# Attention of two of four batches by 32-query chunks instead of 64-query blocks

## The chip, the core and the metric

The kernel runs on one core of one Trainium2 chip. The metric is the time on the device in microseconds (us). An execution has five engines that run side by side: TensorE (PE, with its weight loads shown apart as PEld), VectorE (DVE), ScalarE (ACT), GpSimd (POOL) and SyncE (SP, which here only issues transfers). Each takes its instructions strictly in the order in which the program gives them; engines wait for one another by semaphores.

## The reference

Four batches, 8 heads, 768 positions, head width 64. Queries go in chunks of 32: a chunk sees 8 memory keys, the 16 positions before it, its own 32 and the 8 after it, cut off at the two ends of the sequence. After the attention comes a Fourier mixing over positions and model width, then a two-layer MLP on the normalised sum.

```
for c in range(24):                                   # chunk 32, left 16, right 8
    keys = [mem_k (8), k[max(0, 32c-16) : min(768, 32c+40)]]
    a = softmax(q[32c:32c+32] @ keys.T / 8);  x[32c:32c+32] = a @ [mem_v (8), v[same]]
u = x + real(fft(fft(x, axis=1), axis=2))
un = (u - mean) / sqrt(var + 1e-6)
out = u + relu(un @ w_ch1) @ w_ch2                    # 512 -> 2048 -> 512
```

## The kernel before

**Order of the work.** The program is a list of some hundreds of tasks, each with an engine, a cost in us, the tasks it needs (`after`), the buffers it takes and gives back, and a rank. A planner (`Plan.order`, L114) plays them through by these costs and writes one fixed order per engine; `shortest` (L1432) draws 24 slightly shuffled rankings and keeps the one whose planned end is earliest. So any change of a cost or a dependence reorders every engine. `behind=` says that a task may only be placed once another one has been placed; `lag` lets it be placed that long before its inputs are expected. MLP matmuls have the lowest rank, so they fill what the attention and Fourier tasks leave free on PE.

**Attention.** A task group `attention(n)` (L972) handles one pair of heads; n = 4b to 4b+3 are the four pairs of batch b. In batches 0 to 2, q and k are loaded by POOL's queue (`e_load_qk`, L368), turned by PE (`e_turn_q`, `e_turn_k`) and copied out of PSUM; in batch 3 (`TURNED`) they are loaded in two transfers each of 128-byte pieces and turned by transfers on SP's queue (`e_flip_q`, L408, `e_flip_k`). `e_kT` (L438) spreads k into `kTb`: 12 blocks of 64 queries, each with a column of 128 key slots: 32 unused, 8 memory keys, 88 context keys. `e_scores` (L454) does six blocks of both heads, 12 matmuls of 64 rows by 128 columns with 64 query columns moving; the two heads sit on the two row halves of the array and write to different PSUM banks. `e_exp` (L465) makes two activations of it, one for each 32-query half, with a bias that masks the keys that half may not see. `e_values` (L473) multiplies the exponentials (128 keys by 64 queries, fp32, as weights) by the value rows (65 columns: 64 and a column of ones that gives the sum), 12 matmuls for each half of the pair, two column halves of the array in turn. `e_norm` (L489) divides. Scores and exponentials run twice a pair, values once with 24 matmuls.

**Values.** `e_load_v` (L380) fills one of four buffers `va` in seven transfers on SP's queue, in rows of 256 bytes: 64 + 80 x 11 + 8 x 11 + 8 x 12 = 1,128 rows a head.

**After the attention of a batch** come `e_rows_out` on POOL's queue (L591), `e_rows_turn` on SP's (L595, the task `t_x2`) and `e_mirror` on POOL's (L600, `t_xr`), which bring half of the rows back in reverse order, and beside them the Fourier chain on DVE, ACT and PE (`fourier(b)`: zy L517, pq L524, ff L534, hi L542, lo L547, rows L557, columns L727, sums and statistics L733 to L742), the normalised rows `un` (L752) and their transposes by SP (`e_flip`, L776). Then the MLP of the batch runs in three thirds: layer 1 (`e_ch1`, L803, then relu L812) and layer 2 (L821; in batches 2 and 3 by products with sums on DVE, L858, L870, L875). The loads for batch 3 stand behind transfers of batches 1 and 2 by `behind=` in `attention`.

Of the kernel before, what the change touches and what calls it, by code (L numbers as in the profile page):

```python
# [11 lines left out]
FP32 = mybir.dt.float32  # L12
BF16 = mybir.dt.bfloat16
# [4 lines left out]
CHUNK = 32  # L18
# [4 lines left out]
MEM0 = 32  # L23
OWN = MEM0 + NMEM + LEFT


# [11 lines left out]
class Plan:  # L38
# [18 lines left out]
    def add(self, engine, cost, emit, after=(), take=(), give=(), rank=None, moved=0.0,  # L57
            loose=False, late=0.0, filler=False, behind=None, lag=0.0, pick=None, grain=0.1, head=1.0):
        t = dict(engine=engine, cost=cost, emit=emit, after=[a for a in after if a is not None],
                 take=take, give=give, rank=len(self.tasks) if rank is None else rank,  # L60
                 moved=moved, done=None, at=None, no=len(self.tasks), loose=loose,
                 late=late, filler=filler, behind=behind, lag=lag, pick=pick, grain=grain, head=head)
        self.tasks.append(t)
        return t
# [50 lines left out]
    def order(self):  # L115
# [9 lines left out]
        while any(waiting.values()):  # L125
# [5 lines left out]
            for e, ts_ in waiting.items():  # L131
# [3 lines left out]
                for t in ts_:  # L135
# [4 lines left out]
                    if any(a["done"] is None  # L140
# [3 lines left out]
                        continue  # L144
                    if t["behind"] is not None and t["behind"]["at"] is None:
                        continue
# [59 lines left out]
def kernel(  # L206
# [18 lines left out]
    NHT = DFF // P  # L225
    NT = S // 64
    RB = 8
# [42 lines left out]
    kU = [spool.tile([P, KR + S + KR], BF16, name=f"kU{i}") for i in range(NKU)]  # L270
    kTb = [spool.tile([P, NT, P], BF16, name=f"kTb{i}") for i in range(NKT)]

# [23 lines left out]
    sv = cpool.tile([P, 3], FP32)  # L296
    svS = cpool.tile([P, 3], FP32)
    svD = cpool.tile([P, 1], FP32)
    zero = cpool.tile([P, 1], FP32)
# [5 lines left out]
    mhalf = cpool.tile([P, NST], FP32)  # L305
    mbias = cpool.tile([P, 2], FP32)
    NEG = -BIGM / 8.0
# [20 lines left out]
    def e_masks():  # L328
        nc.gpsimd.memset(mbias, 0.0)
        nc.gpsimd.memset(mbias[96:128, 0:1], NEG)  # L330
        nc.gpsimd.affine_select(out=mbias[:, 1:2], in_=mbias[:, 1:2], compare_op=ALU.is_ge,
                                fill=NEG, base=-(OWN - LEFT + CHUNK), pattern=[[0, 1]],
                                channel_multiplier=1)
        nc.gpsimd.memset(mbias[0:MEM0, 1:2], 0.0)
        nc.gpsimd.memset(mbias[MEM0:MEM0 + NMEM, 1:2], 0.0)
# [11 lines left out]
    def e_edge_ones(i):  # L347
        v1 = va[i]
        lo, hi = v1[32:64, :, 0, D:D + 1], v1[96:128, :, NT - 1, D:D + 1]
        nc.gpsimd.affine_select(out=lo, in_=lo, compare_op=ALU.is_ge, fill=0.0, base=32 - OWN,  # L350
                                pattern=[[0, 2], [0, 1]], channel_multiplier=1)
        nc.gpsimd.affine_select(out=hi, in_=hi, compare_op=ALU.is_ge, fill=0.0,
                                base=OWN + 63 - 96, pattern=[[0, 2], [0, 1]],
                                channel_multiplier=-1)
        nc.gpsimd.memset(v1[MEM0:MEM0 + NMEM, :, 0, D:D + 1], 1.0)

    def e_low_rows(i):
# [22 lines left out]
    def e_load_v(n):  # L380
# [3 lines left out]
        def run(p0, count, t0, nt, key, hh):  # L384
# [3 lines left out]
                                      ap=[[D, count], [64 * D, nt], [1, D]]))  # L388

        nc.sync.dma_start(v1[OWN:OWN + 64, :, 0, 0:D],  # L390
                          v[b, 2 * pr:2 * pr + 2, 0:64].rearrange("h p d -> p h d"))
# [42 lines left out]
    def e_mkT(n):  # L434
        b, pr = seq[n]
        (nc.scalar.copy if n == HP else nc.vector.tensor_copy)(
            kTb[n % NKT][:, :, MEM0:MEM0 + NMEM],
            mkT[:, b * HP + pr, :].unsqueeze(1).to_broadcast([P, NT, NMEM]))  # L438

    def e_kT(n, eng=None):  # L440
        if n >= TURNED * HP:
            win = LEFT + 64 + RIGHT
            nc.vector.tensor_copy(
                strided(kTb[n % NKT], MEM0 + NMEM, [[P, NT], [1, win]]),
                strided(kU[n % NKU], KR - LEFT, [[64, NT], [1, win]]))
            return
        trk = tr_of.pop((n, 1))
        (eng or nc.scalar.copy)(
            strided(kTb[n % NKT], MEM0 + NMEM, [[P, NT], [RB, 11], [1, RB]]),
            strided(trk, 0, [[64 // RB, NT], [1, 11], [KP, RB]]))  # L450
        if n < HP:
            let_go(trk)

    def e_scores(n, g):  # L454
        qT, kT = qT_of[n], kTb[n % NKT]
        sc_of[n, g] = sc = aps.tile([P, 2, 8, 64], FP32, tag="sc", bufs=1, name="sc")
        for t6 in range(6):
            t = 6 * g + t6
            for hh in range(2):
                r0 = 64 * hh  # L460
                nc.tensor.matmul(sc[:, hh, t6, :], kT[r0:r0 + 64, t, :],  # L461
                                 qT[r0:r0 + 64, ts(t, 64)], start=True, stop=True,
                                 tile_position=(r0, 0))

    def e_exp(n, g):  # L465
# [41 lines left out]
    mid32 = cpool.tile([P, NST, 1], FP32)  # L507
    warm = cpool.tile([P, 1], FP32)
    xd, xt = (nc.dram_tensor(name, [2, 3, P, DM], FP32).ap() for name in ("x_rows", "x_back"))
    od = nc.dram_tensor("out_rows", [2, 3, P, DM], FP32).ap()  # L510
    gate = cpool.tile([P, 1], FP32)

# [403 lines left out]
    for i in range(NV):  # L916
# [4 lines left out]
                       rank=(0, 1, 2, 3)[i])  # L921
    t_masks = add("POOL", 0.86, e_masks, rank=16)
    dz = cpool.tile([P, P], BF16)
    fill_of = []
# [43 lines left out]

    t_used = {}

    def attention(n):
# [5 lines left out]
                      take=(("qs", "ks")[i],), moved=3.1 if b >= TURNED else 1.2, grain=0.032 if b >= TURNED else 0.1, late=LATE if b else 2.0,  # L977
                      behind=t_gate if n == HP else t_xr[b - 2] if n == TURNED * HP else t_ck.get(n - 1),
                      rank={0: -4 + i, 1: -1.2 + 0.1 * i, 2: 10 + 0.1 * i}.get(n)) for i in range(2)]
        lv = add("SP", 2.5, lambda: e_load_v(n), [t_ones[n] if n < NV else None, t_used.get(("va", n % NV))],  # L980
                 behind=t_x2.get(b - 2),
                 take=("va",), moved=2.6, grain=0.031, head=0.4, late=(0.0, 4.0, LATE, LATE)[b])
        t_lv[n] = lv
        t_ck[n] = lk
        if n == HP - 1:
# [13 lines left out]
        else:  # L999
# [6 lines left out]
                     take=(ktag,), give=("ks",))  # L1006
            ek = add(dve[0], 1.25 if dve[1] else 1.04, lambda: e_kT(n, dve[1]), [tk, mk],
                     give=(ktag,))
        t_used[0, at], t_used[1, at] = (eq, tk) if b >= TURNED else (tq, tk)
        xs_ = []  # L1010
        for g in range(2):
# [75 lines left out]
    for i in range(2, NV):  # L1087
        t_low[i]["behind"] = t_exp[i - 2, 1]
        t_low[i]["rank"] = t_exp[i - 2, 1]["rank"] + 0.1
# [85 lines left out]
    def fourier(b):  # L1175
        t_x1 = add("POOL", 1.0, lambda: e_rows_out(b), [t_norm[b * HP + i, 1] for i in range(HP)],
                   moved=2.0)
# [29 lines left out]
        return columns_of(b, t_rest)  # L1207

    t_flips = {}

# [199 lines left out]

    t_lv[14]["behind"] = t_x2[TURNED - 1]
    t_lv[15]["behind"] = t_x2[TURNED - 1]

# [33 lines left out]
```

## Time and profile before

| | us |
|---|---|
| runs | 280.25, 280.53, 280.58 (median 280.53) |
| the profiled execution | 280.87 |
| its span, first to last instruction | 279.2 |
| PE busy in the span | 264.8 (95%) |
| DVE, ACT, POOL busy | 192.6 (69%), 154.7 (55%), 63.5 (23%) |
| scores, L461: PE busy, 384 matmuls | 11.6 |
| values, L485: PE busy, xa and xo, 384 records each | 15.4 and 14.5 |
| exponentials, L469: ACT busy, 64 of 580 ns | 33.6 |
| granted TensorE clock | 1.00 |

The profile is one execution. A group's "busy" counts overlapped instructions once, its mean is the latency of one. A matmul's end is modelled and includes the way through the array, so how fast matmuls follow each other is read from starts: in the timeline a run of x records that lasts t and whose single one lasts m has its last start at t - m. One fp32 matmul leaves two records.

### The profile page before, as it was taken

To read this page: it belongs to the slowest core of one execution; us is meant where nothing else is said; L and a number is where in the kernel's file an instruction comes from. 1 tells how busy PE (TensorE), PEld (TensorE's weight loads), DVE (VectorE), ACT (ScalarE), POOL (GpSimd) and SP (SyncE) were. 2 spreads that over 40 slices of the span, in tenths; PEclk is the share of its full clock that TensorE was granted. 3 is DMA by queue.
4 is the path that set the end of the run, shared out by engine and by line. 5 is a ranking of instruction groups with operands and counts; after the bars stand their busy time and mean duration, and the time that the engine had idled before them with its cause. 6 is when DMAs were issued, how large, how long until landed. Compare 5 with 4: busy or idle time off the path is not lost.

```text
span 279.2 us, 7959 instructions
## 1 busy us (share of the span) xinstructions
PE 264.8 (95%) x3318; PEld 208.3 (75%) x3318; DVE 192.6 (69%) x424; ACT 154.7 (55%) x262; POOL 63.5 (23%) x127
## 2 busy tenths in 40 slices
PE   0599999999999999999999999999999999999995
PEld 0387797888765668758767857668889888888884
DVE  7968999941238999999937851259987975353444
ACT  6888647788777527636653556328164191605150
POOL 8852572330201096050211130001100130000000
PEclk9999999999999999999999999999999999999999
DMA  5998999999998999979992586824842057303152
GB/s 95 209 177 159 184 191 203 196 198 194 197 198 216 122 226 165 139 193 156 268 162 78 109 137 178 152 78 137 98 183 40 0 96 149 97 38 77 54 100 76
DMA packets 116116, 39.98 MB, mean 143 GB/s; under 512 B 104560, under 2 KB 111472, under 8 KB 116080
## 3 DMA queue, kind: packets, MB, share of 16 engines
q1 hardware_dynamic: 93888, 23.54, 45.6%
q0 software_dynamic: 21472, 15.21, 33.3%
q10 hardware_dynamic: 720, 0.72, 0.7%
q8 instruction: 26, 0.43, 0.7%
q14 instruction: 10, 0.08, 0.1%
HBM read 37.36 MB, written 13.37 MB: 182 GB/s over the span
## 4 chain that ended last, share of the span: by engine, by line
PE 82%; DVE 6%; POOL 5%; DMA 2%; ACT 2%; issue 2%; POOLq 0%; DVEq 0%
PE ph L803 26%; PE pc L821 15%; PE pc L870 11%; PE ps L557 6%; PE pm L727 5%; PE xa L485 4%; PE xo L485 4%; PE ps L716 3%; PE sc L461 3%; DMA qs<-in_q_dram 2%; PE trq L405 2%; PE trk L405 1%; PE idle L930 1%; ACT un L752 1%; PE pm L608 1%
## 5 line engine op out<-in xcount | busy, mean ns | idle before, releaser
L803 PE MATMUL ph<-unT,w_sb 128*128 128x256 f16 x768 | 90.0, 273 | 0.2 <-ACT hT L812 0.2
L812 ACT ACTIVATE hT<-ph 128x512 f16<-128x512 f32 x96 | 56.8, 597 | 47.3 <-PE ph L803 27.5
L803 PEld LDWEIGHTS <-w_sb 128*128 128x128 f16 x768 | 73.6, 98 | 10.8 <-issue 0.8
L821 PE MATMUL pc<-w_sb,hT 128*128 128x512 f16 x192 | 44.7, 380 | 0.0
L469 ACT ACTIVATE e<-sc,mbias 128x384 f32<-128x384 f32 x64 | 33.6, 580 | 17.7 <-PE sc L461 17.7
L821 PEld LDWEIGHTS <-hT 128*128 128x128 f16 x192 | 17.6, 98 | 19.2 <-issue 0.2
L870 PEld LDWEIGHTS <-hT 128*128 128x128 f16 x240 | 23.3, 98 | 3.9 <-issue 1.0
L875 DVE TENSOR_TENSOR xsb<-pc,xsb 128x256 f32<-128x256 f32 x43 | 17.8, 420 | 9.6 <-PE pc L870 8.4
L870 PE MATMUL pc<-w_sb,hT 128*128 128x256 f16 x192 | 24.1, 273 | 0.2 <-DVE xsb L875 0.2
L828 DVE SCALAR_TENSOR_TENSOR xsb<-pc,rstd,xsb 128x512 f32<-128x512 f32 x12 | 9.0, 749 | 18.8 <-PE pc L821 18.8
L569 ACT CAST up<-ps 128x386 f16<-128x386 f32 x16 | 9.7, 603 | 21.4 <-PE ps L557 20.4
L741 DVE BATCH_NORM_STATS2 st<-xsb 128x6 f32<-128x512 f32 x24 | 16.5, 687 | 0.5
L858 DVE TENSOR_TENSOR S<-hT 128x768 f16<-128x768 f16 (+1 forms) x12 | 5.1, 424 | 16.4 <-ACT hT L812 15.8
L485 PEld LDWEIGHTS xa<-va,e 128*64 128x64 f32 x384 | 13.1, 143 | 3.6 <-issue 2.9
L485 PE MATMUL xa<-va,e 128*64 128x65 f32 x384 | 15.4, 232 | 0.0
L752 ACT ACTIVATE un<-xsb,rs 128x512 f16<-128x512 f32 x12 | 9.5, 807 | 10.1 <-POOL rs L767 10.1
L485 PE MATMUL xo<-va,e 128*64 128x65 f32 x384 | 14.5, 227 | 0.0
L461 PEld LDWEIGHTS <-kTb 64*128 64x128 bf16 x384 | 7.7, 97 | 8.0 <-issue 5.3
L485 PEld LDWEIGHTS xo<-va,e 128*64 128x64 f32 x384 | 13.0, 142 | 0.4 <-ACT ff L651 0.3
L542 ACT CAST hi<-ff 128x768 f16<-128x768 f32 x12 | 9.9, 830 | 4.9 <-DVE ff L534 4.7
L461 PE MATMUL sc<-qT,kTb 64*128 64x64 bf16 x384 | 11.6, 196 | 0.9 <-POOL va L345 0.9
L870 PE MATMUL pc<-w_t,S 128*128 128x256 f16 x96 | 11.6, 272 | 0.4 <-DVE xsb L875 0.4
(168 smaller groups left out, 442.3 us busy)
## 6 DMA issues: line engine op xcount, KB each, us to landing
va<-in_v_dram SPq DMA_DIRECT2D x32, 220.0 KB
w_sb<-in_moe_w_ch_dram POOLq DMA_DIRECT2D x8, 512.0 KB, 14.5
out_dram<-xsb SPq DMA_DIRECT2D x12, 256.0 KB
qs<-in_q_dram POOLq DMA_DIRECT2D x12, 192.0 KB, 6.7
ks<-in_k_dram POOLq DMA_DIRECT2D x12, 192.0 KB, 6.7
x_rows<-xsb POOLq DMA_DIRECT2D x3, 768.0 KB, 4.6
xr<-x_back POOLq DMA_DIRECT2D x3, 768.0 KB, 6.0
out_rows<-xsb SPq DMA_DIRECT2D x9, 256.0 KB
```

The source lines that it names most:

```text
L461: nc.tensor.matmul(sc[:, hh, t6, :], kT[r0:r0 + 64, t, :], qT[r0:r0 + 64, ts(t, 64)], start=True, stop=True, tile_position=(r0, 0))
L469: nc.scalar.activation(e1[:, :, :, ts(half, 32)], sc[:, :, 0:6, ts(half, 32)], AFT.Exp, bias=mbias[:, half:half + 1], scale=1.0 / math.sqr ...
L485: nc.tensor.matmul(xa[64 * half:64 * half + 64, st, hh, 0:65], e1[:, hh, t6, :], v1[:, hh, 6 * g + t6, 0:65], start=True, stop=True)
L557: nc.tensor.matmul(out_[:, sp, :], part[:, ab, sp * 3 + st, c0:c1], tab[:, sp, st, :], start=(st == 0 and i == 0), stop=(st == 2 and i == 1))
L727: nc.tensor.matmul(pm[:, par, :], lhs, rhs[:, par, :], start=(im == 0), stop=(im == 3))
L741: nc.vector.bn_stats(st6, xs[b][:, kt, :])
L752: nc.scalar.activation(un, xs[b][:, kt, :], AFT.Identity, bias=rs[:, 1:2], scale=rs[:, 0:1])
L803: nc.tensor.matmul(ph[:, k, :], w1_sb[:, dt, ts(HH * k + i, P)], unT_of[b, j][:, dt, :], start=(dt == 0), stop=(dt == NDT - 1))
L812: nc.scalar.activation(hT_of[b, j][:, :, i, :], ph, AFT.Relu, bias=0.0, scale=1.0 if b in EVEN else -1.0)
L821: nc.tensor.matmul(pc_of[b, j, r], hT_of[b, j][:, k, i, ts(r, P)], w2_sb[:, HH * k + i, :], start=(i + k == 0), stop=(i + k == HH))
L870: nc.tensor.matmul(pc_of[key], a[:, i, :], w[:, i, :], start=(i == 0 and new), stop=(i == HH - 1), skip_group_check=not new)
L875: nc.vector.tensor_tensor(u, pc, u, ALU.add)
```

## The change

For the pairs n >= 8 (`FINE`: batches 2 and 3) the unit is the chunk of 32 queries with 64 keys: 56 context and 8 memory keys.

- **Scores and exponentials.** 48 matmuls of 64 by 64 with 32 columns moving, in one task; even and odd chunks go to the two partition halves. One activation over 768 columns without bias. The keys lie chunk after chunk with the memory keys between two windows, so that an odd chunk has them after its window, an even one before.
- **Values.** 48 fp32 matmuls with 64 rows by 32 columns of weights; eight in a row go to eight different places of the array. Both heads of one 128-row tile no longer share a bank: head 0 goes to xa, head 1 to xo. The norm is by head.
- **Value loads.** For each head two runs of 56-row windows and one of the memory rows (kept twice in a scratch tensor that two transfers on ACT's queue write at the start): 56 x 24 + 16 x 12 = 1,536 rows a head. At the first and last pair one window more is loaded apart. The windows of the two end chunks reach past the sequence; POOL multiplies these blocks by 0 or 1 (`e_cut`), and PE's values wait for that.
- **New small tasks.** `e_edge` on POOL once, `e_ones` on ACT once for each of the four buffers before its first use by batch 2.
- **Order of loads.** The q and k loads of n = 14 also stand behind `t_xr[2]`; the value load of 12 stands behind the last `e_flip` of batch 1, those of 13, 14 and 15 behind `t_x2[2]` (before: 12 and 13 behind `t_x2[1]`, 14 and 15 behind `t_x2[2]`).

```diff
-    kTb = [spool.tile([P, NT, P], BF16, name=f"kTb{i}") for i in range(NKT)]
+    kTf = [spool.tile([P, NCH * 64 + NMEM], BF16, name=f"kTb{i}") for i in range(NKT)]
+    kTb = [x[:, 0:NT * P].rearrange("p (t k) -> p t k", k=P) for x in kTf]
...
+    def e_cut(n):
+        ends = va[n % NV][:, :, 0:NT:NT - 1, 0:D + 1]
+        nc.gpsimd.tensor_tensor(ends, ends, edge.unsqueeze(3).to_broadcast([P, 2, 2, D + 1]), ALU.mult)
...
+        if n >= FINE:
+            for hh in range(2):
+                lo, hi = ((0, 64 + NMEM), (64 + NMEM, 0))[hh]
+                alone = hh == 0 and pr == 0
+                run(lo, WIN, alone, NT - alone, 64 * alone - LEFT, hh)
+                if alone:
+                    run(lo + LEFT, WIN - LEFT, 0, 1, 0, hh)
+                alone = hh == 1 and pr == HP - 1
+                run(hi, WIN, 0, NT - alone, CHUNK - LEFT, hh)
+                if alone:
+                    run(hi, WIN - RIGHT, NT - 1, 1, S - CHUNK - LEFT, hh)
+                two = mem2[b, 2 * pr + hh].rearrange("i m d -> (i m) d")
+                nc.sync.dma_start(v1[WIN:WIN + 2 * NMEM, hh, :, 0:D],
+                                  two.unsqueeze(1).to_broadcast([2 * NMEM, NT, D]))
+            return
...
+    def half_of(c, hh):
+        return 64 * ((c + hh) % 2)
+
+    def f_scores(n):
+        sc_of[n] = sc = aps.tile([P, 2, 16, CHUNK], FP32, tag="sc", bufs=1, name="sc")
+        for c in range(NCH):
+            for hh in range(2):
+                r0, p0 = 64 * hh, half_of(c, hh)
+                k0 = 64 * c + (0 if p0 else NMEM)
+                nc.tensor.matmul(sc[p0:p0 + 64, hh, c // 2, :], kT[r0:r0 + 64, k0:k0 + 64],
+                                 qT[r0:r0 + 64, ts(c, CHUNK)], start=True, stop=True,
+                                 tile_position=(r0, p0))
+
+    def f_exp(n):
+        nc.scalar.activation(e1, sc[:, :, 0:NT, :], AFT.Exp, scale=1.0 / math.sqrt(D))
+
+    def f_values(n):
+        for st in range(NST):
+            for c4, hh in ((0, 0), (1, 0), (2, 0), (3, 0), (1, 1), (0, 1), (3, 1), (2, 1)):
+                c = 4 * st + c4
+                p0, c0 = half_of(c, hh), CHUNK * c4
+                nc.tensor.matmul(xa[hh][c0:c0 + CHUNK, st, 0:65],
+                                 e1[p0:p0 + 64, hh, c // 2, :], v1[p0:p0 + 64, hh, c // 2, 0:65],
+                                 start=True, stop=True, tile_position=(p0, c0))
...
     def attention(n):
-                      behind=t_gate if n == HP else t_xr[b - 2] if n == TURNED * HP else t_ck.get(n - 1),
+                      behind=[t_gate if n == HP else None if n == TURNED * HP else t_ck.get(n - 1)] + [{"x": t_xr, "v": t_lv}[k].get(i) for k, i in {12:[('x',1)],14:[('x',2)]}.get(n, ())],
...
-                 behind=t_x2.get(b - 2),
-                 take=("va",), moved=2.6, grain=0.031, head=0.4, late=(0.0, 4.0, LATE, LATE)[b])
+                 behind=[{"x": t_x2, "m": t_xr, "v": t_lv, "f": {z: t_flips[z][5] for z in t_flips}}[k].get(i) for k, i in {12:[('f',1)],13:[('x',2)],14:[('x',2)],15:[('x',2)]}.get(n, ())],
+                 take=("va",), moved=3.7 if fine else 2.6, grain=0.031, head=0.4, late=(0.0, 4.0, LATE, LATE)[b])
+        if fine:
+            cut = add("POOL", 0.55, lambda: e_cut(n), [lv, t_edge], lag=CUT)
...
+        if fine:
+            s_ = add("PE", 0.45, lambda: f_scores(n), [eq, ek], take=("sc",), give=("qT", "kTb"))
+            x_ = add("ACT", 0.98, lambda: f_exp(n), [s_], take=("e1",), give=("sc",))
+            v_ = add("PE", 0.95, lambda: f_values(n), [x_, cut], take=("xa",), pick=vp, give=("e1", "va"))
...
-    t_lv[14]["behind"] = t_x2[TURNED - 1]
-    t_lv[15]["behind"] = t_x2[TURNED - 1]
```

## The prediction

> **What bounds the kernel.** I read the page first: busy shares, the 40 slices, the chain.
>
> ```profile
> PE 264.8 (95%) x3318; PEld 208.3 (75%) x3318; DVE 192.6 (69%) x424; ACT 154.7 (55%) x262; POOL 63.5 (23%) x127
> ...
> PE   0599999999999999999999999999999999999995
> ...
> PE 82%; DVE 6%; POOL 5%; DMA 2%; ACT 2%; issue 2%; POOLq 0%; DVEq 0%
> ```
>
> PE is at 9 tenths in every slice from the third to the last but one, at full clock; no other engine is. So after some 14 us every microsecond of PE work counts, as long as there is other PE work to put in its place. The same by stage (columns: window, its length, then busy us of PE, PEld, DVE, ACT, POOL, each with its instruction count, clock, DMA share, GB/s):
>
> ```profile
> 70.00:115.00 45.00, 45.00 (x752) 31.95 (x752) 32.88 (x64) 28.12 (x46) 13.40 (x18) 1.00 1.25 187
> 115.00:147.00 32.00, 31.77 (x275) 22.66 (x273) 26.45 (x48) 18.37 (x31) 6.49 (x8) 1.00 1.12 185
> 147.00:187.00 40.00, 40.00 (x471) 27.45 (x469) 18.91 (x43) 18.69 (x32) 4.73 (x12) 1.00 0.54 118
> 187.00:235.00 48.00, 47.43 (x445) 41.87 (x442) 41.94 (x89) 23.05 (x38) 5.71 (x14) 1.00 0.47 102
> 235.00:277.00 42.00, 40.95 (x371) 36.01 (x369) 18.73 (x45) 14.33 (x24) 0.00 (x0) 1.00 0.31 76
> ```
>
> Attention of batches 2 and 3 lies in the first three. The DMA engines are full until 147 (share over 1, as packets of several queues overlap), then half so. From 187 to 235 PE does the MLP of batch 2 beside the Fourier part of batch 3, in which DVE is nearly as full as PE. From 235 on only the MLP of batch 3 is left.
>
> **What PE gives for one pair now.** The last pair, in the timeline of PE (start, length, line, count):
>
> ```profile
> 180.40 0.35 PE L461 MATMUL sc<-qT,kTb 64*128 64x64 bf16 x12
> 180.68 1.90 PE L821 MATMUL pc<-w_sb,hT 128*128 128x512 f16 x8
> 182.51 0.35 PE L461 MATMUL sc<-qT,kTb 64*128 64x64 bf16 x12
> 182.79 0.61 PE L821 MATMUL pc<-w_sb,hT 128*128 128x512 f16 x2
> ...
> 185.49 0.92 PE L485 MATMUL xa<-va,e 128*64 128x65 f32 x24
> 186.24 0.87 PE L485 MATMUL xo<-va,e 128*64 128x65 f32 x24
> 187.04 0.50 PE L803 MATMUL ph<-unT,w_sb 128*128 128x256 f16 x3
> ```
>
> One score block holds PE from 180.40 to 180.68: 0.28. One of its matmuls lasts 0.19 (the tile's median), so the twelfth starts at 0.16; two run side by side on the row halves, so one place takes a matmul every 0.16/5.5 = 0.029, and 0.12 goes into leaving the block. Entering costs too: a pc matmul lasts 0.38, so the last one ahead starts at 180.68 + 1.90 - 0.38 = 182.20 and the block at 182.51, 0.31 later, against 0.61 - 0.38 = 0.23 between two pc matmuls: 0.09, rounded up. Two blocks: 2 x 0.37 = 0.74. The values hold PE from 185.49 to 187.04: 1.55. In the second half 24 records have their last start at 0.87 - 0.22 = 0.65; two column halves side by side give 12 slots, 0.65/11 = 0.058 each, and the way out costs 0.80 - 12 x 0.058 = 0.10.
>
> **What it gives after.** Scores: 48 matmuls on four places, 12 slots. A slot costs at most the 0.029 of now (the moving columns are halved) and at least half of it: 0.17 to 0.35, plus 0.12 and 0.09, in all 0.38 to 0.56. I take 0.49, nearer the known row. Saved 0.25. Values: 96 records on eight places, 12 slots. The trace has two row halves side by side (scores) and two column halves (values), not both at once nor four columns. If all eight run side by side: 0.75 as for the first half now, 0.05 until the eighth place has started, 0.10 to leave, 0.90; saved 0.65. If only two do: 48 slots, 1.55 + 24 x 0.058 = 2.94; lost 1.39. If four do: 24 slots as now; saved nothing. I take eight, since each kind of halving shows its full gain alone and the streams of one place keep their length (65 columns, 0.058). The sum is 8 pairs x (0.25 + 0.65) = 7.2 us of PE.
>
> Two rules of the Trainium skill speak against it. The first: "TensorE: Matmul & The Clock Gate" (Part 1) states that start-to-start never falls below about 25 ns, however small a matmul is. In the rows above twelve score matmuls start within 0.16 us, 14 ns apart, so here it can hold for one place only; were it one floor for all, 48 + 96 starts would by estimate take 3.6 us a pair against the 2.29 of now, and the sum would be some 10 us slower than before. The second: "TensorEngine Tiling (Array Packing)", Gotcha 1 (PSUM Pressure), states that different row tiles cannot access the same PSUM bank at the same time. No run here shows it: the scores keep each row half in its own bank, but the new values write each bank from both row halves, in different column quarters. If that serialises, four places run side by side and only the scores' 2.0 us are left.
>
> **The other engines.** ACT: four exponentials of 0.580 (128x384) become one of 768 columns; the cast L542 of 768 takes 0.83, so about 0.9: 1.4 saved a pair. ACT is not full (28, 18 and 19 us of 45, 32, 40), so this is latency: the second score block and its exponentials, 182.51 - 180.40 = 2.1 us, leave the way from k to values. `e_kT` grows from 1,056 to 1,344 columns: 0.28 more on ACT (1.04 a copy), 0.12 more on DVE (0.425), and memory-key copies double (0.22): beside that, nothing. The norm keeps its sizes (0.557 and 0.187). `e_ones` and the two scratch transfers stand early on ACT, with a buffer free at 52 us whose load is issued at 68.6: nothing; without that room 0.3 us each.
>
> `e_cut` has no equal in the trace. POOL's 128x2 power takes 0.71, its 128x800 memset 0.77, a 128x3 sum 0.35: between 0.3 and 1.5 us, 0.7 taken. It lies between landing and values; value loads of the last pairs are issued by 88 (values at 112) and by 161.5 (values at 185.5), so it has some 15 us of cover even after a landing of 7 (q and k loads take 6.7 to 7.7 from issue). Behind it on POOL wait q and k loads, x_rows and the mirror; more of that among the rivals.
>
> **Loads.** A pair's value rows rise from 2,256 to 3,072. Queue q1 takes 45.6% of 279.2 = 127 us for 93,888 packets, so 8 x 816 more cost about 8.9 us of all DMA engines, half of it before 147 where they are full. Against that two value loads (2 x 2,256 packets, 6 us) and the q, k loads of n = 14 leave that stage. One issue fewer a pair on SP (0.3 to 0.6) is nothing. Batch 3's loads now all come after 140, when x_rows of batch 2 is turned: 3 x 3,072 value rows and 4 x 1,536 rows of q and k are 15,400 packets, at 93,888/127 = 739 a microsecond 21 us, so until about 161. Before, the last k was flipped by SP at 169.1 and value load 15 issued by 161.5. So the loads come about when they came: 0, between 5 us earlier and 8 later for the attention's end.
>
> **The sum.** PE is relieved by 7.2 us before 187. From there the filler has to last: the first third of batch 3's MLP starts at 235.14, and the transposes it needs are issued at
>
> ```profile
> 228.05 2.53 SPq L776 DMA_TRANSPOSE unT<-un  x2
> ```
>
> the first of these two ends its issue near 229.3; with some 2 us to land (estimate; plain transfers take 4.6 to 7.7 from issue) it is there at about 231, 4 us before PE comes to it. With the 2.1 us by which the last attention gets shorter, 6 us of PE's lead can be used: the smaller of 7.2 and 6.1, so 6.0. 280.87 - 6.0 = 274.9 for the profiled execution; the median lies 0.34 below it: **274.5**.
>
> **Rivals.**
> - Capped by Fourier (17%): the lead is used up at 231 because batch 3 comes no earlier, or up to 3 us later: gain 1 to 4, 276.5 to 279.5. For it: DVE at 41.9 of 48. Against: it does not wait for loads now.
> - More (7%): the whole 7.2 and less stalling of the planned orders: 272 to 273.
> - The places do not run side by side (slower, 9%): f_values takes 48 slots, 8 x (1.39 - 0.25) = 9 us more: 289.5. It decides once the values need more than 24 + 0.25/0.058 = 28 slots, under 3.4 places at a time. At four places it is 280.5 - 2.0 = 278.5, inside the range and counted with the capped case.
> - Late batch 3 (slower, 11%): `e_cut` of 12 and 13 stands on POOL ahead of q and k loads of 14 and 15, waits for value loads that only start at 140, and the last k lands late. With an end of attention later by d the MLP of batch 3 waits d - 4 us: slower from 4 us on; at 8, 284.5.
> - No effect (5%): the order the planner finds gives back what PE gains; within 0.2%, which is what a measurement here can tell from no change.
> - The forecast, 51%: 273 to 276.5.
>
> Faster 0.51 + 0.17 + 0.07 = 0.75, same 0.05, slower 0.20. The range goes from the "more" case to a mild late batch 3: 271.8 to 282.
>
> **What would show it.** Right: a score block at 0.5 and a value block at about 0.9 from first start to the next line, PE still at 9 everywhere, the first third of batch 3's MLP at about 229. Wrong: value slots over 0.058 or a block of 1.5 and more; PE idle before layer 1 of batch 3 with a flip as releaser; POOL waiting long for a value load with q or k loads behind; exponentials far over 0.9.

## The result, and the profile after

The changed kernel takes 287.2 us (median of six runs, 285.93 to 288.37) against 280.5 for the kernel before beside it (280.21 to 280.92): 1.0238 times as long, with an interval of 1.0207 to 1.027. It is slower, on the other side of the forecast of 274.5 and above its range. The profiled execution took 285.93, with a span of 284.2, 5.0 us more than before. Its runs also lie 2.4 us apart, against 0.7 before. Below, a median and a ratio leave out runs that are over 1.5% above the fastest of their kernel.

The page of the changed kernel, in the same three rows as before (busy time, PE in 40 slices, chain that ended last):

```profile
PE 261.3 (92%) x3894; PEld 204.7 (72%) x3894; DVE 195.2 (69%) x424; ACT 148.0 (52%) x242; POOL 71.4 (25%) x143
...
PE   0599999999999999999997999968899998999995
...
PE 64%; DVE 23%; POOL 5%; issue 4%; DMA 2%; ACT 0%; POOLq 0%; DVEq 0%
```

PE is busy 3.5 us less, and nothing is won by it: the row of slices is no longer a row of nines. There are holes in the 22nd slice and from the 27th to the 29th, a small one in the 34th (a slice is 7.1 us long). PE's records went up from 3,318 to 3,894. The chain has 23% of DVE instead of 6, and 4% instead of 2 of "issue", an engine that waits for nothing that the profile shows.

The stages of the changed kernel (window, length, busy us of PE, PEld, DVE, ACT, POOL with counts, clock, DMA share, GB/s):

```profile
115.00:147.00 32.00, 32.00 (x371) 22.30 (x370) 27.51 (x52) 15.75 (x26) 9.15 (x11) 1.00 0.93 165
147.00:187.00 40.00, 37.44 (x573) 25.94 (x572) 17.92 (x39) 16.72 (x27) 8.00 (x18) 1.00 1.20 168
187.00:235.00 48.00, 43.26 (x572) 37.46 (x570) 38.20 (x81) 19.60 (x32) 5.04 (x10) 1.00 0.44 99
```

From 147 to 187 PE now stands for 2.56 us, and before for none; from 187 to 235 for 4.74 us, and before for 0.57. The same window has a DMA share of 1.20 where it was 0.54: batch 3's loads and its larger value rows now lie there. What PE waited for (engine and line, what released it, us in all, times, longest):

```profile
PE ph L892 <- issue: 2.8, 2, 1.4
PE pc L959 <- DVE xsb L964: 2.4, 4, 1.0
PE xa L540 <- issue: 1.6, 1, 1.6
PE sc L523 <- issue: 1.0, 1, 1.0
```

5.4 us in four stops have the releaser "issue". The kernel before has no such stop after its start-up. All four lie on the chain that ended last. Two of them there, in order of time (start, length, what):

```profile
153.46 1.53 PE ph L892 x14
154.99 1.40 issue
156.39 2.13 PE ph L892 x18
...
188.98 1.60 issue
190.58 0.25 PE xa L540 x3
```

The first stands in the middle of 32 matmuls of layer 1 whose operands are all there, the second 13 records before the end of a value block, which a block that had begun can't owe to its inputs. The other two are 0.96 at 185.59, within a score block, and 1.40 at 194.09, within layer 1.

**What PE ran out of.** The page's row of the instruction queue reads 30 packets and 0.49 MB now, 26 and 0.43 MB before: 16 KB a packet. 6,636 records of PE and PEld go with 26 packets, 7,788 with 30: some 256 instructions of PE each. (The count below takes in 66 and 61 records more of PE's sequencer, semaphore waits above all.) So the place at which the next packet is asked for comes back every 256 instructions. I set it, from the trace, at the earliest place of any packet among the six before and the six behind, and counted from there: how long until the packet starts, and how many PE instructions have run when PE stops.

| kernel, packet that starts at | us after its due place | PE instructions since then, at the packet's start | when PE stops | stop begins, PE goes on (after packet's start) |
|---|---|---|---|---|
| before, 109.69 (its worst) | 4.06 | 176 | - | no stop |
| after, 113.92 | 3.85 | 242 | - | no stop, 279 when it was there |
| after, 153.94 | 5.59 | 264 | 280 | 154.99, +2.45 |
| after, 184.10 | 3.07 | 235 | 282 | 185.59, +2.45 |
| after, 187.80 | 2.51 | 115 | 282 | 188.98, +2.78 |
| after, 193.07 | 4.46 | 162 | 282 | 194.09, +2.42 |

PE stops each time at the same count, 280 to 282 instructions past the due place, and goes on about 2.5 us after the packet's start. That is what running out of instructions looks like: PE has used up the 256 that were left to it (and some 25 by which my due place is early), and the next block is still on its way. In the kernel before the count never came beyond 241 from 65 us on, up to 2.4 us after a packet's start.

### The profile page after: what moved, and what is told of

Read it like the earlier page. It is cut to its first block, busy times and chain, and to the rows that moved or that the text cites. A ratio compares the mean times of both kernels' runs of the same rounds, so it can differ in the third digit from the quotient of the medians.

```text
span 284.2 us, 9120 instructions
## 1 busy us (share of the span) xinstructions
PE 261.3 (92%) x3894; PEld 204.7 (72%) x3894; DVE 195.2 (69%) x424; ACT 148.0 (52%) x242; POOL 71.4 (25%) x143
## 4 chain that ended last, share of the span: by engine, by line
PE 64%; DVE 23%; POOL 5%; issue 4%; DMA 2%; ACT 0%; POOLq 0%; DVEq 0%
PE ph L892 24%; PE pc L910 11%; PE pc L959 9%; PE pm L816 3%; PE ps L805 3%; DVE lo L636 2%; DVE ff L623 2%; DVE zy L606 2%; PE ps L646 2%; DVE st L830 2%; DVE xsb L964 2%; DMA ks<-in_k_dram 2%; PE xa L576 2%; PE xo L576 2%; DVE pq L613 1%
## 5 line engine op out<-in xcount | busy, mean ns | idle before, releaser
L560 ACT ACTIVATE e<-sc,mbias 128x384 f32<-128x384 f32 x32 | 16.8, 579 | 4.5 <-PE sc L509 4.5
L482 DVE COPY kTb<-mkT 128x200 bf16<-128x200 bf16 (+1 forms) x15 | 3.9, 290 | 15.9 <-PE sc L509 8.4
L386 POOL TENSOR_TENSOR va<-va,mbias 128x260 f32<-128x260 f32 x8 | 6.2, 779 | 34.0 <-DMA va<-mem_twice 30.8
L822 DVE TENSOR_TENSOR xsb<-pm,xsb 128x512 f32<-128x512 f32 x15 | 10.0, 672 | 4.9 <-PE pm L816 4.8
L606 DVE TENSOR_TENSOR zy<-xsb 128x768 f32<-128x768 f32 x12 | 12.3, 1028 | 0.2
L623 DVE TENSOR_TENSOR ff<-pq 128x762 f32<-128x762 f32 x12 | 11.3, 942 | 0.0
L408 POOL DMA_DIRECT2D ks<-in_k_dram x12 | 7.8, 646 | 14.0 <-PE trk L451 10.8
```

What stands on the lines that cost most here:

```text
L560: nc.scalar.activation(e1[:, :, :, ts(half, 32)], sc[:, :, 0:6, ts(half, 32)], AFT.Exp, bias=mbias[:, half:half + 1], scale=1.0 / math.sqr ...
L606: nc.vector.tensor_tensor(zy_of[b, par][:, :, c0:c0 + P], xb[:, :, c0:c0 + P], xb[:, :, HD + c0:HD + c0 + P], ALU.add if par == 0 else ALU ...
L623: nc.vector.tensor_tensor(ff[:, ab, :, 1:P], pq[:, :, 1:P], rev_ap(pq, HD - 1, P - 1, [[HD, NST]]), op)
L822: nc.vector.tensor_tensor(uv, pm_of[b, kt], uv, ALU.add)
```

## The experiments

Each edit is against the changed kernel if nothing else is said. "Before" was run beside all of them, at 280.56 to 280.88. What is said of stops is read from one profiled execution of each kernel.

**The order of the loads.** Two runs part the loads from the arithmetic.

```diff
 # e1_old_loads: only these two lists
-{12:[('x',1)],14:[('x',2)]}                              # q and k loads
+{12:[('x',1)]}
-{12:[('f',1)],13:[('x',2)],14:[('x',2)],15:[('x',2)]}    # value loads
+{12:[('x',1)],13:[('x',1)],14:[('x',2)],15:[('x',2)]}
 # e2_new_loads_only
-    FINE = 8
+    FINE = 16
```

> The changed kernel with batch 3's loads in the order of before (value loads 12 and 13 behind the turned rows of batch 1, 14 and 15 behind those of batch 2; the q and k loads of 14 no longer behind the mirror of batch 2). Theory 'late loads' (batch 3's last pairs come late because their loads do): the last attention ends near 186 instead of 195 us in the span, 276 to 280 us. Theory 'instruction fetch' (PE runs out of instructions in the dense runs of small matmuls; four holes of 1.0 to 1.6 us sit on the chain): holes of over 1 us stay wherever two pairs stand close, in all 3 to 5 us, 282 to 286. Theory 'unlucky order' (the planner's draw, not the change): anything, with no link to either.

Measured: 291.7 us (two runs), ratio 1.0396 (1.0364 to 1.0428), 4.5 us worse than the change. So the later loads of batch 3 don't cost the change its gain; with the chunked attention they are the better order. The chunked attention met a stop of 3.8 us at 89, 280 instructions past the due place, with a packet that started 4.06 us late. Its stops come to 5.3 us, as in the changed kernel; beside them layer 1 waited 3.8 us in six times for the relu on ACT.

> The attention of before for all batches, with the changed kernel's order of batch 3's loads (only the constant that switches the chunk attention on is set past the last pair). Late loads: 283 to 287, the last attention ends some 5 us later than the 189 of before. Instruction fetch: no holes on PE, 280 to 281.5.

Measured: 282.77, ratio 1.011 (1.0057 to 1.0164), with no stop of "issue". The count past the due place stays under 225. With the attention of before, the order of the loads costs 2.2 us; the rest of the loss comes with the chunked attention. With that attention the same order is a gain, as e1 shows, so the 2.2 can't simply be added to the rest.

**Fewer instructions with the same loads.** In bf16 a matmul takes two PE instructions instead of the four of fp32, so these kernels read the upper halves of the same floats. The array time falls as well: a value block of 96 records holds PE for 1.11 us, one of 48 for 0.48.

```diff
 # x1_bf16_values (x2_bf16_all: without the condition)
-                nc.tensor.matmul(xa[hh][c0:c0 + CHUNK, st, 0:65],
-                                 e1[p0:p0 + 64, hh, c // 2, :], v1[p0:p0 + 64, hh, c // 2, 0:65],
+                w_, m_ = e1[p0:p0 + 64, hh, c // 2, :], v1[p0:p0 + 64, hh, c // 2, 0:65]
+                if n >= 12:
+                    w_, m_ = w_.bitcast(BF16)[:, 1::2], m_.bitcast(BF16)[:, 1::2]
+                nc.tensor.matmul(xa[hh][c0:c0 + CHUNK, st, 0:65], w_, m_,
```

> The changed kernel in its own order on every engine, but the 48 value matmuls of each pair of batch 3 read only the upper halves of the fp32 numbers as bf16: half the PE records, a quarter of the passes; so batch 3's values lose precision. Instruction fetch: the holes of PE at 185 to 196 us shrink from 4.0 to under 1.5 us, 2.5 to 4.5 us faster than the changed kernel, 282.5 to 284.5. Late loads: only the shorter value blocks show, 0.3 us each on the way, holes stay: 0.5 to 1.5 faster, 285.5 to 287.

Measured: 283.59, ratio 1.0102 (1.0069 to 1.0135), 3.6 us less than the change. The stops between 185 and 196 are gone. So are 2.5 us of array time in four value blocks, so the 3.6 are not the stops alone. But two stops of 1.5 us and one of 0.5 came up in batch 2, whose program is the changed kernel's and which had none in its profile: whether a packet comes in time differs from run to run, which would fit the wider spread too. And the last attention still ends at 195.2, as its next limit shows in the chain:

```profile
137.12 4.05 SPq L687
...
147.30 3.45 SPq L460
...
150.86 8.08 DMA va<-in_v_dram
```

SP's queue and batch 3's value loads are on the chain here, with 6% and 9% of the span, where the changed kernel had PE. Behind the stops lay a second limit: the loads.

> The changed kernel in its own order, with the value matmuls of all pairs of batches 2 and 3 on the upper halves of the fp32 numbers as bf16, so these lose precision; the run with batch 3 alone took 283.6 against 287.2. Instruction fetch: batch 2's holes go as well, 279.5 to 282. If the shorter blocks alone had made the first gain of 3.6: the same again, 280. If what is left is batch 3's late end: 282.5 to 284.

Measured: 281.8, ratio 1.0034 (1.0008 to 1.0061). A little less again. The profiled execution, at 285.24 the longest of the nine, has stops of 2.2 and 1.1 us; 96 instructions of scores and 96 of values are still 192 a pair, against 144 before.

**The draw of the plan, and the rows.**

```diff
 # s1_other_draws
-            draw = random.Random(found[1] if i is None else i)
+            draw = random.Random((found[1] if i is None else i) + 100)
 # x3_fewer_rows, in e_load_v
-                alone = hh == 1 and pr == HP - 1
-                run(hi, WIN, 0, NT - alone, CHUNK - LEFT, hh)
-                if alone:
-                    run(hi, WIN - RIGHT, NT - 1, 1, S - CHUNK - LEFT, hh)
```

> The changed kernel with 24 other draws of the planner (seeds 100 to 123). Unlucky order: over 2 us away from the 287.2 of the changed kernel, perhaps under 281. Late loads and instruction fetch: 285 to 289, with the last attention again ending after 192.

Measured: 285.6 (two runs, 284.63 and 286.57), ratio 1.0178 (1.0134 to 1.0222). An unlucky draw is not the cause: another plan is slower than before as well. Its profile, taken at 288.94, has stops too (3.4, 1.9 and 0.3 us of "issue"), partly at other places, at counts from 269 to 288.

> The changed kernel in its own order, but the second of the two value runs of each head is left out for batches 2 and 3 (its partitions keep old values, so their attention is wrong): 864 rows a head instead of 1,536, under the 1,128 of before. PE gets the same instructions. Fetches late because DMA is loaded: holes on PE under half of the 6 us, 280 to 284. Fetches late because of PE's density alone: the holes stay, 285.5 to 288.

Measured: 285.33, ratio 1.0165 (1.0123 to 1.0206). With the second run of each head's value rows left out the stops come to 3.0 us instead of 5.4: the transfers seem to have a part in them, but not the whole. Two profiles alone can't say how large a part, since x1 showed that stops come and go between runs.

**Instructions without the change.** The kernel before gets more PE instructions and nothing else.

```diff
 # x4_tiny_matmuls: before, behind the values of each pair of batches 2 and 3
+        for i in range(72 if n >= 8 and g == 1 else 0):
+            c0 = 32 * (i % 4)
+            nc.tensor.matmul(xa[c0:c0 + 32, i % 3, 0, 65:66], dz[0:64, 0:32], dz[0:64, 0:1],
...
 # m1_burst: before, in e_ch1 (x in range(512), few is a PSUM tile of its own)
+        if (b, j, i) == (3, 1, 0):
...
+                nc.tensor.matmul(few[c0:c0 + 32, x % 2, 0, 0:1], dz[r0:r0 + 64, 0:32],
+                                 dz[r0:r0 + 64, 0:1], start=True, stop=True,
...
 # m2_calm_bursts: the same with x in range(96), and
+        if b == 3 and i in (1, 6):
```

> The kernel before, in its own order on every engine, with 72 matmuls of one column (zero weights, into an unused column of the value bank) behind the values of each pair of batches 2 and 3: 144 PE instructions more a pair, as many as the change adds, no byte of DMA more. The extra matmuls by themselves should hold PE 0.7 to 1 us a pair, 6 to 8 us in all, so 286 to 289. Instruction fetch by count alone: beside that, holes of over 0.5 us on PE in the profile, 2 us or more in sum after 60 us, and 288 to 293. Instruction fetch only where DMA is loaded more as well: no such holes, 285 to 288.5. Other causes (load order, planned order): no holes.

Measured: 293.77, ratio 1.0459 (1.0395 to 1.0523): holes as "by count alone" had them, the time a little above its range. In the timeline of PE the stop falls into a score block of the old kind (the last column in brackets is the idle time and what ended it):

```profile
108.13 0.87 PE L485 MATMUL xo<-va,e 128*64 128x65 f32 x24
108.93 0.70 PE L490 MATMUL xo<-dz 64*32 64x1 bf16 x72
109.56 0.29 PE L461 MATMUL sc<-qT,kTb 64*128 64x64 bf16 x7
113.25 0.32 PE L461 MATMUL sc<-qT,kTb 64*128 64x64 bf16 x5 [3.40 <-issue]
```

Seven of twelve score matmuls run, then PE stands for 3.4 us, 271 instructions past the due place; the packet started at 110.79, 4.17 us late. No load, no plan and no exponential had been changed. The other stop, of 1.0 us, came behind a row of small matmuls, 268 instructions past a due place whose packet started only 0.88 us late:

```profile
92.49 0.70 PE L490 MATMUL xo<-dz 64*32 64x1 bf16 x72
93.12 0.35 PE L461 MATMUL sc<-qT,kTb 64*128 64x64 bf16 x12
93.40 0.32 PE L405 MATMUL trq<-ident_b,qs 96*64 96x96 bf16 x5
94.67 0.41 PE L405 MATMUL trq<-ident_b,qs 96*64 96x96 bf16 x11 [0.96 <-issue]
```

Of the 11.4 us by which this span is longer, the extra matmuls took 5.0 (0.63 a block until the next line starts), the two stops 4.4, and layer 1 (L807) is busy for 1.8 more; the granted clock was 0.80 from 114 to 125 us.

> The kernel before with 512 matmuls of one column (64 rows by 32 columns of zero weights, all eight places in turn) at the start of the second third of batch 3's MLP, where DMA is at three tenths: 1,024 PE instructions in a row. If instructions come 256 at a time and some 2.4 us after a request: three or four stops of 1 to 2.5 us within the burst, 6 to 11 us for it. If PE can issue as fast as the value blocks do (10 ns a matmul with its load): one piece of 4 to 6 us without stops of over 0.5 us.

Measured: 295.53 in one run beside 280.85. The 512 matmuls in the timeline of PE:

```profile
248.06 1.73 PE L805 MATMUL few<-dz 64*32 64x1 bf16 x196
251.96 1.17 PE L805 MATMUL few<-dz 64*32 64x1 bf16 x128 [2.18 <-issue]
255.96 1.18 PE L805 MATMUL few<-dz 64*32 64x1 bf16 x128 [2.83 <-issue]
259.69 0.61 PE L805 MATMUL few<-dz 64*32 64x1 bf16 x60 [2.55 <-issue]
```

This is the cleanest picture of the cause. After the first stop PE runs exactly 128 matmuls, 256 instructions, in 1.17 us and stands again. The packets start 3.80 and 3.55 us apart. So PE takes 256 instructions in 1.2 us if it has them, and gets 256 in about 3.7 us, even where the DMA engines are nearly empty (a share of 0.07).

> The kernel before with six runs of 96 matmuls of one column (192 PE instructions each, as many as a value block of the changed kernel has) in the MLP of batch 3, two in each third, some 5 us apart, where the DMA engines are at 3 tenths or less. It tells whether the density of PE instructions alone makes the stops, or only together with loaded DMA engines. In the traces so far the packet that brings the next 256 PE instructions starts some 0 to 1.5 us after it is due where the DMA engines are calm, 2 to 6 us where they are full. If both are needed: packets start within 1.5 us of their due place here, no stop with releaser issue over 0.5 us, and the time is that of the extra matmuls alone, six times about 1 us: 286 to 288 us. If density alone does it, as in the run of 1,024 instructions: two to four stops of 1 to 3 us, 290 us and more.

Measured: 286.0, ratio 1.0193 (1.0172 to 1.0213). Blocks as dense as a value block of the change make no stop where the DMA engines are calm:

```profile
236.60 0.90 PE L805 MATMUL few<-dz 64*32 64x1 bf16 x96
237.43 4.54 PE L810 MATMUL ph<-unT,w_sb 128*128 128x256 f16 x40
241.90 0.90 PE L805 MATMUL few<-dz 64*32 64x1 bf16 x96
242.73 1.92 PE L810 MATMUL ph<-unT,w_sb 128*128 128x256 f16 x16
```

No packet started more than 1.71 us after its due place, and the count stayed under 200. The six blocks hold PE for 0.83 us each, 5.0 of the 5.35 us. So a block of 192 instructions within a microsecond doesn't stop PE by itself where the packet comes in time and large matmuls follow. PE stops when it has used up its instructions before the next packet is there. A late packet brings that about, and so do more small matmuls behind the block (m1; the shorter stop of x4). Full DMA engines make a packet late, but a stop just before it can do so too: before the last stop of the changed kernel the packet started 4.46 us late while DMA was almost idle (share 0.06, the last figure but one):

```profile
188.60:193.10 4.50, 2.90 (x106) 2.29 (x90) 1.95 (x5) 0.91 (x3) 0.00 (x0) 1.00 0.06 17
```

PE had gone on from the stop before at 190.58, and that packet started 2.5 us later. In all traces here no two packets start less than 3.3 us apart.

**Halving, spreading, and relief without instructions.**

```diff
 # y2_batch3_only
-    FINE = 8
+    FINE = 12
 # y3_values_in_thirds: f_values(n, part) does two of the six row groups;
 # for PE tasks with a lag the plan now also spaces PE tasks
-            v_ = add("PE", 0.95, lambda: f_values(n), [x_, cut], take=("xa",), pick=vp, give=("e1", "va"))
+            v_ = add("PE", 0.32, lambda: f_values(n, 0), [x_, cut], take=("xa",), pick=vp)
+            v_ = add("PE", 0.32, lambda: f_values(n, 1), [v_], lag=0.3)
+            v_ = add("PE", 0.32, lambda: f_values(n, 2), [v_], lag=0.3, give=("e1", "va"))
 # y1_before_bf16: the kernel before, in e_values
+                    w_, m_ = e1[:, hh, t6, :], v1[:, hh, 6 * g + t6, 0:65]
+                    if n >= 8:
+                        w_, m_ = w_.bitcast(BF16)[:, 1::2], m_.bitcast(BF16)[:, 1::2]
```

> The changed kernel with the chunked attention in batch 3 alone (FINE = 12), its order of loads kept. By the supply of PE instructions the loss goes with the number of dense pairs: the new loads alone had taken 282.8, all eight pairs 287.2, so four pairs give about 285 (284 to 286), with stops of issue only from batch 3's attention on, 2 to 4 us in sum. The rival, that it is batch 3's late attention alone that costs and batch 2's pairs give a net gain: 287 to 289 us.

Measured: 286.33, ratio 1.0197 (1.0158 to 1.0235; its runs from 284.13 to 288.01). Half the pairs cost nearly as much as all, above my 284 to 286 and below the rival's 287: one stop of 3.3 us at its first dense pair, 272 instructions past a due place whose packet came 5.19 us late. So the loss doesn't go by the number of dense pairs alone; in the profiled run it is one pair that met a late packet.

> The changed kernel, same instructions, but each pair's values are planned as three tasks, each at least 0.3 us (plus the plan's own slack of 0.7) behind the one before, so that other matmuls come between. If the stops come from the density of PE instructions over a microsecond or two, they shrink: issue under 3 us in sum, 283 to 285 us. If it is the mere number of instructions, or something else in these blocks, nothing is gained: 286 to 289 us, with stops as before. Each exit from a block costs some 0.1 us, 16 more of them 1.6 us, in both cases.

Measured: 291.09, ratio 1.0369 (1.033 to 1.0409). The run doesn't tell what I wanted of it. Two stops of "issue" of 1.6 us each are left, but the pairs hold their buffers longer, the last attention ended at 205, and PE then waited 5.8 us for the transposes of batch 3 (unT<-un). The new plan costs more than the stops that went.

> The kernel before, in its own order of work; the value matmuls of batches 2 and 3 read the upper halves of the same floats as bfloat16, so both the array time and the number of PE instructions of these blocks fall (24 float32 matmuls, 96 instructions a pair, become 48 instructions). The probabilities and values lose precision; nothing else is changed. If the stops of the changed kernel came from the supply of PE instructions, and relief of PE can otherwise be turned into time as I had summed, this kernel shows it: a value pair falls from 1.55 us to some 0.6 to 0.8, 8 x 0.8 = 6 to 7 us of PE work less with fewer instructions, no stop with releaser issue over 0.5 us, and 274 to 277 us. The rival, that the lead of PE can't be used at all, since the Fourier part of batch 3 on DVE or the loads set the end: 278.5 to 280.5 us, with the relief showing as waits of PE for DVE between 187 and 240.

Measured: 276.3, ratio 0.9835 (0.9814 to 0.9857), faster than both kernels, at the price of the precision of values and probabilities. A value block falls from 1.55 to some 0.53 us; the eight blocks hold PE for 4.5 us instead of 12.4, 7.9 less, and the span is 4.9 us shorter. Its chain and its PE row:

```profile
PE   0499999999999999799999999998999999999995
...
PE 64%; DVE 15%; POOL 6%; DMA 5%; ACT 4%; issue 3%; SPq 1%; POOLq 0%; DVEq 0%
```

It has no stop of "issue" on PE over 0.5 us, and its count stays under 214. So less PE work does become time in this kernel, about 0.62 of it; the rest goes into PE's waits, for DVE (1.3 us) and for ACT (1.0) above all.

## Why the prediction was wrong

- **What bounds the kernel** was right: PE. y1 shows it.
- **Values, eight places side by side**: right in kind. The 96 records of a block start within 0.96 us, about 10 ns apart. But a slot takes 0.083 us ((0.96 - 0.05)/11) and not the 0.058 that I took as unchanged, and the block holds PE for 1.10 us, not 0.90: a saving of 0.45 and not 0.65. Why a place is slower among eight is not shown.
- **Scores**: the block holds PE for 0.49 us, in the timeline of PE:

```profile
144.35 0.56 PE L523 MATMUL sc<-qT,kTb 64*64 64x32 bf16 x48
144.84 0.61 PE L892 MATMUL ph<-unT,w_sb 128*128 128x256 f16 x4
```

  That is the 0.49 that I took, but by luck: mine had 0.09 for the entry in it, which this one has not, and a slot takes 0.38/11 = 0.035, more than the 0.029 that I had as the most. With the entry on both sides it is 0.58 against 0.74: 0.16 saved, and not 0.25.
- **The relief** was therefore mis-sized. The eight value blocks hold PE for 9.2 us without their stops, and 12.4 before; the scores for 4.4 and 4.5. That is 3.3 us, or 4.0 with eight entries fewer, instead of 7.2.
- **Two rules of the Trainium skill.** The floor of 25 ns between starts ("TensorE: Matmul & The Clock Gate", Part 1) doesn't hold over all places of the array: 10 ns here. The rule on banks ("TensorEngine Tiling (Array Packing)", Gotcha 1) doesn't show: both row halves wrote one bank, in different column quarters, and were not serialised. That would by estimate take 24 x 0.058 + 0.10 = 1.5 us a block, and 1.10 were measured. I looked at the two rules that didn't matter, and not at the one that did. "Runtime: NRT & Kernel Launch", section "Instruction fetch mechanics", states that an engine's instructions come in blocks of 16 KiB, 256 of them, with the next one fetched while one is worked off. Both agree with the packets here. It adds that crossing a block is mostly hidden, as instructions leave more slowly than they come. m1 shows the contrary for PE: 1.17 us to use a block, 3.7 to get one.
- **`e_cut` and the other engines**: right. 0.64 us (median) against 0.7, and PE waited for it once, for 0.4 us. An exponential of 768 columns takes 0.81 us (0.9 taken).
- **Loads, "0" taken from between 5 earlier and 8 later**: it was 6.7 later. The last value load leaves SP at 175.1 instead of 161.5, and the last attention ends at 195.9 instead of 189.2. 4 of these 6.7 us are the three stops at 185, 189 and 194; the new order of loads alone puts it at 191.3 (e2).
- **The sum is the step that failed**: "6 us of PE's lead can be used". I priced a block by the time for which the array holds it and counted its instructions at nothing. A pair has 96 for scores and 192 for values instead of 48 and 96, and 5.4 us of stops came from it, on a PE that has no slack. Some more is given back between 196 and 238, where the late Fourier part of batch 3 makes PE wait 2.4 us for DVE, and 0.6 before: the case that I had called capped by Fourier.
- **The rivals.** None had the cause. The slower one, late batch 3, named a wrong way to it: POOL issues the q and k loads of the last two pairs from 142.0 to 149.3, right behind the mirror of batch 2, and the next `e_cut` comes after them.

The two profiles add up so: PE is busy 3.5 us less and stands 8.5 us more, 5.4 of them in the stops, 1.8 more in waits for DVE, 1.3 in smaller ones; that makes the 5.0 by which the span is longer. What the kernel would take without stops was not measured: x1 and x2 also shorten the array's work.

Not shown is what holds a packet back. Over the 14 traces, from 65 us on, the median packet started 2.3 us after its due place where the DMA share ahead of it was 1 or more (133 packets), and 0.9 us where it was under 0.8 (131, without the last three of m1's burst). The first median is the higher one in each of the traces, but single packets lie anywhere from 0 to 9 us. Whether a packet waits behind others on one DMA engine was not tried.

## What to carry to other kernels

Small matmuls on parts of the array cost instructions as well as array time: count both, for each microsecond in which they come. Here PE got 256 instructions in 3.3 to 3.8 us at best, some 70 to 80 a microsecond, and its small matmuls used some 200 a microsecond. Once it was some 250 to 290 instructions past the place at which the next packet was due, it stopped. The sign of it is idle time with the releaser "issue" in the middle of a group whose inputs are all there. Before halving a tile, look in the trace at how late those packets start, where DMA queues are full above all.

## What the runs showed of the hardware

- PE's instructions came in packets of 16 KB, some 256 each, and PE's 28 stops of "issue" over 0.25 us in these runs came 249 to 295 instructions past the due place, 25 of them at 268 and more (the place is set by the trace, so it is not exact). It went on 2.2 to 3.1 us after the packet's start.
- In m2 a packet started within 1.7 us of its due place where the DMA engines were at 3 tenths; where they were full, packets of all traces came 0 to 6 us after it, now and then up to 9. Behind a stop they came up to 4.5 us late with idle DMA engines as well (after, m1).
- The clock that PE is granted was lower behind some of the stops. In m1, with stops of 2.2 to 2.8 us:

```profile
244.00:248.00 4.00, 3.99 (x37) 3.29 (x34) 2.83 (x7) 0.00 (x0) 0.00 (x0) 1.00 0.00 0
248.00:262.00 14.00, 6.44 (x523) 5.63 (x522) 0.42 (x1) 0.00 (x0) 0.00 (x0) 0.66 0.07 23
262.00:270.00 8.00, 8.00 (x57) 6.41 (x56) 0.43 (x2) 3.58 (x6) 0.00 (x0) 0.75 0.31 68
```

The clock is at 0.66 over the stretch with the stops and still at 0.75 in the 8 us behind it, in which PE is busy throughout. The one-column matmuls without a stop left it at 0.998 over the whole of m2. In the changed kernel, with stops of at most 1.6 us, it stayed at 1.00, in y2 with one of 3.3 us too. In x4 it was at 0.77 and 0.80 with one of 3.4 us and behind it, and in y3 it was low behind one of only 1.6 us that ended at 86.4:

```profile
87.00:91.00 4.00, 4.00 (x26) 1.46 (x25) 1.49 (x4) 0.85 (x2) 0.63 (x1) 0.59 1.09 221
```

So the length of one stop alone doesn't decide it; what does is not shown.
